# Clustered attention with two feed-forward blocks: tied clusters to the general path, four operand stacks, 15 fp32 probability steps, a new placement table

## The chip, the cores and the metric

The kernel runs on one core of one Trainium2 chip. The metric is device time in microseconds (us) of one execution, by the median of three runs.

## The reference

Sixteen heads (two batches of eight) of 768 tokens and 64 features go through attention in which a query sees only the keys of its own cluster. The result is the input of two feed-forward blocks.

```python
q_assign = np.argmax(einsum(q_n, c_n)); k_assign = np.argmax(einsum(k_n, c_n))   # 16 clusters
scores = np.where(q_assign == k_assign, (q @ k.T) / 8, -1e9)                     # 768 x 768 per head
attn = softmax(scores);  x = attn @ v                                            # (2, 768, 512)
u = x + real(fft2(x));  un = layernorm(u)
x = u + relu(un @ w_ch1) @ w_ch2                                                 # 512 -> 2048 -> 512
h = relu(x @ w_in);  out = (h * sigmoid(conv3(h))) @ w_out                       # 512 -> 1024 -> 512
```

`argmax` takes the first of several equal maxima.

## The kernel before, in words

The program holds the network twice. The fast path (`general=False`) runs first and computes a flag `fits` on the way (`heads_fit`, L692): the inputs' sizes lie in the ranges that its fp16 splits allow, and every query has a key in its cluster. If the flag is 0, the general path runs after it. All that follows is the fast path.

**Stages.** Attention with everything around it; the first feed-forward block for batch 0, then for batch 1; the second block. Values that need more than fp16 are split into a high and a low fp16 part, and a product is three matmuls (`pass3`).

**The attention loop** runs over 96 steps n, six per head: step n takes 128 keys of head n // 6 and all 768 queries. The query and key operands of a head, with 16 rows of cluster mask and a row for the maxima, lie in a pair of tiles X and Y, a *stack*. There are three stacks, used in turn (`Xs[h % 3]`). In program order a step does this:

- `score_max(n + LEAD)`, LEAD = 8: two matmuls make the scores of a step eight ahead (L1049, tile `s`), and VectorE takes the maximum of each row (L1056, `m6all`). When a head's six are there, `max_turn` (L1059) turns them round on TensorE, ScalarE scales them (L1064, `mr`), and a DMA puts them as one row into the head's stack (L1065, X<-mr). It is placed at step 6h - 2, two steps before the head h needs it.
- `score_exp(n)`: four matmuls make the transposed scores less the maxima (L1103 from X, L1105 from Y, tile `t`), ScalarE takes the exponential (L1112) into an fp32 tile `p`, of which there are three.
- `prob_hi(n - 1)` and `prob_lo(n - 1)`: the high part of p by a cast (ScalarE L1130, VectorE L1128 for steps in CAST_ON_DVE), the low part by a subtraction (GpSimd L1140, VectorE for steps in LO_ON_DVE).
- `attn_v(n - 4)`: 18 fp16 matmuls with the values (L1159). A *whole* step, by WHOLE = (2, 5) two steps of each head up to step 89, has no cast and no subtraction and takes six fp32 matmuls instead (L1152; the profile counts each twice). There are 29 of them; three more (IN_PLACE) leave p in PSUM.

The `s` and `t` tiles share three PSUM slots in turn (`slot`), so that TensorE can begin the next score only when VectorE's maximum or ScalarE's exponential has emptied an earlier one.

**Around the loop.** For each pair of heads m: loads (`load_raw`, `load_v`), the split of q and k (`prep_hi` L946, `prep_lo` L959, all on VectorE), similarity to the centroids (`prep_sims`), the maximum (L847) and a one-hot (L857) which holds several ones where clusters tie. For the first pair three VectorE operations pick the first of them (`prep_first` L861, `prep_pick` L865, `prep_mark` L871), for the other pairs two small matmuls with the matrix `sole` do (`equal_sole` L899, ScalarE L903, VectorE L906). The masks go to the stacks by way of DRAM (`equal_end`, `stack_mask`). From step 52 on the Fourier mixing of batch 0 (`mixing`, called stages `even0` to `ab2M`), its layer norm and the bits of four weight pieces (`ahead`) lie between the steps.

**What sets the order.** Every engine runs its instructions in the order in which the program issues them. The loop issues a step's parts in a fixed order, with lists between them (`pre`, `mid`, `mid2`, `late`, `aft`, `post`, `fill`); each small operation or load has a list and a step, and the table MOVED overrides these for 136 of them. All loads go out on SP's queue, those of the Fourier matrices (DFT_LOADS) on GpSimd's.

Of the kernel before, what the change touches and what calls it, by code (L numbers as in the profile page):

```python
# [23 lines left out]
DFT_LOADS = (9, 20, 21, 32, 33, 44)  # L24
# [154 lines left out]
    ('load_v', 1): ('late', 1),  # L179
    ('prep_lo', 1, 1): ('late', 1),  # L180
    ('stack_move', 2, 1, 2): ('aft', 2),
    ('v_step', 0, 4): ('aft', 2),
    ('v_step', 0, 6): ('pre', 3),
    ('prep_sims', 2): ('post', 5),
    ('prep_hi20', 2): ('fill', 6),
    ('equal_turn', 2): ('mid', 7),
    ('equal_sole', 2, 0): ('mid', 8),
    ('prep_hi21', 2): ('aft', 8),
    ('equal_sole', 2, 1): ('mid', 9),
    ('prep_lo', 2, 0): ('pre', 9),  # L190
    ('load_v', 2): ('fill', 10),
    ('attn_out', 0, 0): ('pre', 11),
    ('attn_out', 0, 1): ('pre', 11),
    ('prep_lo', 2, 1): ('late', 11),
    ('attn_out', 0, 2): ('fill', 12),
    ('load_raw', 3): ('aft', 12),
    ('v_step', 1, 6): ('pre', 12),
    ('v_step', 1, 4): ('late', 13),
    ('v_step', 1, 5): ('aft', 14),
    ('ahead_start', 0): ('aft', 15),  # L200
    ('ahead0_0',): ('aft', 16),
    ('ahead0_1',): ('fill', 16),
# [4 lines left out]
    ('v_step', 2, 6): ('late', 18),
    ('prep_hi31', 3): ('late', 20),
    ('v_step', 2, 5): ('late', 20),
    ('prep_hi30', 3): ('late', 21),  # L210
    ('attn_out', 2, 1): ('late', 22),
    ('prep_lo', 3, 1): ('pre', 22),
    ('prep_lo', 3, 0): ('late', 23),
    ('ahead0_3',): ('pre', 25),
    ('ahead_start', 1): ('aft', 25),
    ('ahead0_4',): ('fill', 26),
    ('attn_out', 2, 2): ('late', 26),
    ('ahead_split', 0, 0): ('fill', 27),
    ('ahead_store', 0): ('pre', 27),
    ('attn_out', 3, 0): ('aft', 27),  # L220
    ('ahead1_1',): ('fill', 29),
    ('attn_out', 3, 1): ('fill', 29),
    ('prep_sims', 4): ('post', 29),
    ('v_step', 3, 4): ('fill', 29),
    ('ahead1_2',): ('fill', 31),
    ('attn_out', 3, 2): ('fill', 31),
    ('v_step', 3, 5): ('pre', 31),
    ('prep_hi41', 4): ('fill', 32),
    ('prep_lo', 4, 0): ('late', 33),
    ('prep_lo', 4, 1): ('aft', 33),  # L230
    ('attn_out', 4, 1): ('aft', 34),
    ('ahead_start', 2): ('pre', 35),
    ('ahead1_3',): ('fill', 36),
    ('attn_out', 4, 2): ('aft', 36),
    ('ahead1_4',): ('pre', 37),
    ('ahead_split', 1, 0): ('pre', 39),
    ('attn_out', 5, 0): ('aft', 39),
    ('ahead2_0',): ('pre', 40),
    ('v_step', 4, 4): ('fill', 40),
    ('ahead2_1',): ('fill', 41),  # L240
    ('ahead_store', 1): ('fill', 41),
    ('attn_out', 5, 1): ('late', 41),
    ('prep_sims', 5): ('post', 41),
    ('v_step', 4, 6): ('pre', 42),
    ('v_step', 4, 5): ('fill', 43),
    ('prep_hi50', 5): ('pre', 44),
# [1550 lines left out]
```

## Time and profile before

| | us |
|---|---|
| runs of the kernel before | 668.8, 669.81, 675.71 |
| median | 669.81 |
| the profiled execution, its own time | 667.78 |
| its span, first to last instruction | 666.1 |
| around the span | 1.68 |
| TensorE busy in the span | 628.2 |
| VectorE, ScalarE, GpSimd busy | 482.0, 403.9, 121.4 |
| mean granted TensorE clock, of full speed | 0.983 |

In the rows below, PE is TensorE's matmuls, PEld its weight loads, DVE VectorE, ACT ScalarE, POOL GpSimd, SPq the queue of the loads. An arrow reads out<-in. A number in square brackets in a row of the timeline is the time for which the engine was idle before it and what ended that. A row of a stretch has the stretch's length, each engine's busy time in it with the number of instructions, then the granted clock (1.00 is 2.4 GHz, 0.50 is 1.2 GHz), the DMA engines' share and GB/s.

### The profile page before, as it was taken

The page shows a single profiled execution, that of the slowest core. Times are in us where ns is not written, and L with a number is a line of the kernel's source. Part 1 is how long each engine was busy: PE and PEld are TensorE (multiplying, and loading weights), DVE is VectorE, ACT ScalarE, POOL GpSimd, SP SyncE. Part 2 cuts the span into 40 slices and gives each one's busy share as a digit, 9 for nine tenths or more (in the row PEclk, how much of TensorE's full clock was granted, in tenths as well). Part 3 has the DMA queues.
Part 4 walks back from the last instruction along what each step waited for, and adds up shares of the span by engine and source line. Part 5 has one row for each costly group of instructions (what it writes and reads, how often), then busy time and mean ns, then how long its engine had stood idle before and what let it go on. Part 6 is the DMA issues. An engine that isn't in the chain of part 4 may idle for free.

```text
span 666.1 us, 11641 instructions
## 1 busy us (share of the span) xinstructions
PE 628.2 (94%) x4665; PEld 388.5 (58%) x4665; DVE 482.0 (72%) x814; ACT 403.9 (61%) x695; POOL 121.4 (18%) x108
## 2 busy tenths in 40 slices
PE   7799898898999999999999999999999999999995
PEld 3467676676877776565655555555555555555552
DVE  6988786979579998978789428777413489967663
ACT  6577586866477685787468514445413368886652
POOL 3252633644417631000020000000000000000000
PEclk9899798998999999999999999999999999999999
DMA  5445636554121610353034300333200002235202
GB/s 161 123 126 161 191 86 190 142 136 116 47 71 40 192 39 2 126 190 127 1 135 181 127 1 1 127 127 127 95 1 1 0 1 75 92 120 190 96 0 100
DMA packets 21943, 64.39 MB, mean 97 GB/s; under 512 B 7126, under 2 KB 8822, under 8 KB 19064
## 3 DMA queue, kind: packets, MB, share of 16 engines
q1 hardware_dynamic: 20872, 59.81, 28.3%
q0 software_dynamic: 1008, 3.75, 1.9%
q8 instruction: 38, 0.62, 0.4%
q14 instruction: 25, 0.20, 0.1%
HBM read 49.59 MB, written 4.89 MB: 82 GB/s over the span
## 4 chain that ended last, share of the span: by engine, by line
PE 61%; DVE 19%; ACT 12%; DMA 4%; issue 2%; ACTq 0%; DVEq 0%
PE acc L387 7%; PE acc L388 7%; PE acc L389 7%; DVE m6all L1056 5%; PE up L387 4%; PE up L389 4%; PE up L388 4%; PE av L1152 4%; PE t L1103 3%; DMA X<-mr 3%; PE t L1105 2%; PE av L1159 2%; PE s L1049 2%; PE u L387 2%; PE u L389 2%
## 5 line engine op out<-in xcount | busy, mean ns | idle before, releaser
L1112 ACT ACTIVATE p<-t,cbias 128x768 f32<-128x768 f32 x93 | 83.5, 899 | 44.7 <-PE t L1105 44.0
L1140 POOL TENSOR_TENSOR p<-p,p 128x768 f16<-128x768 f32 x47 | 84.9, 1812 | 126.0 <-DVE p L1128 69.7
L1056 DVE TENSOR_REDUCE m6all<-s 128x1 f32<-128x768 f32 x96 | 90.5, 948 | 23.4 <-PE s L1049 14.9
L387 PE MATMUL up<-un,wa 128*128 128x384 f16 x256 | 83.5, 326 | 1.9 <-DVE un L586 0.9
L389 PE MATMUL up<-un,wa 128*128 128x384 f16 x256 | 83.4, 326 | 0.0
L388 PE MATMUL up<-un,wa 128*128 128x384 f16 x256 | 83.4, 326 | 0.0
L1512 DVE SCALAR_TENSOR_TENSOR h<-up,h 128x384 f16<-128x384 f32 x62 | 33.6, 552 | 53.2 <-ACT h L1510 53.0
L387 PE MATMUL acc<-wa,h 128*128 128x512 f16 x186 | 70.6, 380 | 0.0
L388 PE MATMUL acc<-wa,h 128*128 128x512 f16 x186 | 70.5, 379 | 0.0
L389 PE MATMUL acc<-wa,h 128*128 128x512 f16 x186 | 70.5, 379 | 0.0
L1510 ACT ACTIVATE h<-up 128x384 f16<-128x384 f32 x62 | 29.9, 484 | 65.4 <-PE up L389 65.2
L1103 PE MATMUL t<-X 97*128 97x384 f16 x192 | 48.8, 336 | 14.4 <-DVE m6all L1056 8.1
L1159 PEld LDWEIGHTS <-p 128*128 128x128 f16 x1206 | 47.7, 100 | 9.6 <-issue 1.7
L1049 PE MATMUL s<-X 80*128 80x384 f16 x192 | 48.5, 336 | 4.9 <-DVE m6all L1056 4.0
L1159 PE MATMUL av<-V,p 128*128 128x65 f16 x1206 | 49.6, 197 | 0.0
L1105 PE MATMUL t<-Y 128*128 128x384 f16 x192 | 48.9, 337 | 0.0
L1152 PEld LDWEIGHTS av<-V,p 128*128 128x128 f32 x348 | 44.8, 200 | 2.0
L1152 PE MATMUL av<-V,p 128*128 128x65 f32 x348 | 44.2, 279 | 0.0
L387 PE MATMUL u<-x,wb 128*128 128x384 f16 x128 | 41.7, 326 | 0.2
L389 PE MATMUL u<-x,wb 128*128 128x384 f16 x128 | 41.7, 326 | 0.0
L388 PE MATMUL u<-x,wb 128*128 128x384 f16 x128 | 41.7, 326 | 0.0
L387 PE MATMUL acc<-wb,gH 128*128 128x512 f16 x96 | 36.4, 379 | 0.2 <-ACT gH L1548 0.2
(362 smaller groups left out, 1266.5 us busy)
## 6 DMA issues: line engine op xcount, KB each, us to landing
rawa<-w SPq DMA_DIRECT2D x14, 1024.0 KB, 5.4
rawb<-w SPq DMA_DIRECT2D x8, 1024.0 KB
heads<-qk SPq DMA_DIRECT2D x8, 768.0 KB, 5.2
raw<-qk SPq DMA_DIRECT2D x7, 768.0 KB, 6.7
Y<-G SPq DMA_DIRECT2D x27, 192.0 KB, 3.9
vraw<-v SPq DMA_DIRECT2D x8, 384.0 KB, 4.1
heads<-v SPq DMA_DIRECT2D x8, 384.0 KB, 4.2
out<-y SPq DMA_DIRECT2D x12, 256.0 KB, 4.4
```

Of the source, the lines that this page charges most:

```text
L387: T.matmul(o, sH, mH, start=start, stop=False)
L388: T.matmul(o, sH, mL, start=False, stop=False)
L389: T.matmul(o, sL, mH, start=False, stop=stop)
L1049: T.matmul(t[:, c, 0:384], X[0:80, 0, sl], X[0:80, 1, 384 * c:384 * c + 384], start=True, stop=True)
L1056: V.tensor_reduce(m6s[h][:, i:i + 1], t[:, :, 0:384], AX.XY, ALU.max, negate=True)
L1103: T.matmul(t[:, c, 0:384], X[0:rx, 1, sl], X[0:rx, 0, 384 * c:384 * c + 384], start=True, stop=False)
L1105: T.matmul(t[:, c, 0:384], Y[0:ry, k, sl], Y[0:ry, q, 384 * c:384 * c + 384], start=False, stop=True)
L1112: A.activation(p, t[:, :, 0:384], AF.Exp, bias=cbias[:, 0:1], scale=0.125 if general else 0.125 / QK_SCALE ** 2)
L1140: eng.tensor_sub(p16[:, 1], p, p16[:, 0])
L1152: T.matmul(avs[h][:, 65 * j:65 * j + 65], p[:, 128 * j:128 * j + 128], v32[:, WHOLE.index(i), h % 2], start=(i + j == 0), stop=(i == 5), s ...
L1159: T.matmul(o, p16[:, k, 128 * j:128 * j + 128], v16[:, i, h % 2, 65 * part:65 * part + 65], start=(i + j + k + part == 0), stop=(i == 5), ...
L1512: V.scalar_tensor_tensor(h[1][:, tk], o, 0.0, hh, ALU.max, ALU.subtract)
```

## The change

- **Ties.** The fast path no longer picks the first of tied clusters: `prep_first`, `prep_pick`, `prep_mark`, `equal_sole`, `desc` and `sole` go. The one-hot is turned and scaled straight to the mask by two ScalarE operations, the second of which sums its output (`ties`, by `accum_out`). `first_ties` does the sum for the first pair. `heads_fit` tests that the keys have exactly one cluster each, with one more matmul and four more VectorE operations of one column; otherwise `fits` is 0.
- **Four stacks** (`Xs[h % len(Xs)]`), and `prep_stack` may come earlier. `lead(n)` is 8, 9 from step 7 and 10 from step 19 (CATCH_UP), and `max_turn` moves with it, to the first n with n + lead(n) > 6h + 5.
- **WHOLE = (3,)**: 15 fp32 steps instead of 29; 14 more steps have a cast, a subtraction and 18 fp16 matmuls. The tile `pw` has 2 buffers instead of 4, `p16` 7 instead of 8, `raw` 2 instead of 1.
- **Engines.** Four of sixteen `prep_lo` go from VectorE to GpSimd (two operations each there), and the fp32 copy of v (`v_step` 6, now half as large) from ScalarE to GpSimd. Other steps stand in LO_ON_DVE and CAST_ON_DVE: 17 subtractions on VectorE as before, 61 on GpSimd for 47, 18 casts on VectorE for 22, 60 on ScalarE for 42.
- **Places.** MOVED is new, with 237 entries, and DFT_LOADS are at other steps.

```diff
-DFT_LOADS = (9, 20, 21, 32, 33, 44)
+DFT_LOADS = (2, 12, 25, 26, 29, 36)
...
-    ('prep_lo', 1, 1): ('late', 1),
+    ('prep_lo', 1, 1): ('aft', -7),
...
+LOW_ON_DVE = {0, 1, 4, 6, 7, 8, 9, 10, 11, 12, 13, 15}
+CATCH_UP = (7, 19)
...
-WHOLE = (2, 5)
+WHOLE = (3,)
...
+        T.matmul(o[:, 32:40], ones.to_broadcast([128, 128]), ties, start=True, stop=True)
...
-        V.scalar_tensor_tensor(r[:, 5:6].bitcast(I32), r[:, 2:3], most, r[:, 4:5], ALU.is_le, ALU.mult)
+        V.scalar_tensor_tensor(r[:, 6:7], r[:, 2:3], most, r[:, 4:5], ALU.is_le, ALU.mult)
+        V.tensor_scalar(r[:, 7:8], o[:, 32:33], 0.5 - 2 * S * (C - 1), None, ALU.is_le)
+        V.tensor_reduce(r[:, 0:1], o[:, 33:40], AX.X, ALU.max)
+        V.scalar_tensor_tensor(r[:, 7:8], r[:, 0:1], MASK_K * (0.5 - 2 * S * (C - 1)), r[:, 7:8], ALU.is_le, ALU.mult)
+        V.tensor_tensor(r[:, 5:6].bitcast(I32), r[:, 6:7], r[:, 7:8], ALU.mult)
...
+            if not general:
+                o = ohTs[m] = ep.tile([96, 2, 2, 128], F16, tag="ohT", bufs=1, name=f"ohT{m}")
+                o = o.rearrange("p a h n -> p a (h n)")
+                A.activation(o[:, 0], p[:, 0], AF.Copy, scale=MASK_Q)
+                A.activation(o[:, 1], p[:, 1], AF.Copy, bias=-MASK_K, scale=MASK_K, accum_out=ties[0:96, m:m + 1])
+                equal_end(m)
+                return
...
-                A.activation(V32s[m % 2][:, :, :, 0:64], src, AF.Copy, scale=V_SCALE)
+                G.tensor_scalar(V32s[m % 2][:, :, :, 0:64], src, V_SCALE, None, ALU.mult)
...
+        def first_ties():
+            e = eqs[0].rearrange("p (h a n) c -> p h a (n c)", h=2, a=2)[:, :, 1]
+            A.activation(e, e, AF.Copy, accum_out=ties[:, 0:1], bias=-1.0)
...
+        def lead(n):
+            return LEAD + (0 if general else sum(n >= c for c in CATCH_UP))
...
-                at(mid, 6 * h - 2, max_turn, h)
+                at(mid, next(n for n in range(100) if n + lead(n) > 6 * h + 5), max_turn, h)
...
+        if not general:
+            add_stack(G)
+            add_ones(G, 3)
...
-            tile_s = score_max(n + LEAD, mid.get(n, []))
+            for k in range(n + lead(n - 1), n + lead(n) + 1):
+                tile_s = score_max(k, mid.get(n, []) if k == n + lead(n) else [])
```

Three places show how the order moves. On ScalarE around the maxima of head 4 (`mr4`), whose first step is 24 (`p24`), the order was:

```order
L1112 ACTIVATE p20_954<-t20_949,cbias_72 128x768
L946 ACTIVATE G3_957<-raw3_700 128x768
L1112 ACTIVATE p21_995<-t21_990,cbias_72 128x768
L946 ACTIVATE G3_957<-raw3_700 128x768
L1064 ACTIVATE mr4_1012<-s30_1008 6x128
L1130 CAST p16_21_1016<-p21_995 128x768
L1112 ACTIVATE p22_1023<-t22_1018,cbias_72 128x768
L1130 CAST p16_22_1050<-p22_1023 128x768
L1112 ACTIVATE p23_1057<-t23_1052,cbias_72 128x768
L1112 ACTIVATE p24_1094<-t24_1089,cbias_72 128x768
```

On the same engine it now is:

```order
L1178 ACTIVATE mr4_963<-s30_959 6x128
L1248 CAST p16_19_967<-p19_947 128x768
L1230 ACTIVATE p20_974<-t20_969,cbias_72 128x768
L1248 CAST p16_20_999<-p20_974 128x768
L1230 ACTIVATE p21_1006<-t21_1001,cbias_72 128x768
L1230 ACTIVATE p22_1041<-t22_1036,cbias_72 128x768
L1248 CAST p16_22_1068<-p22_1041 128x768
L1230 ACTIVATE p23_1075<-t23_1070,cbias_72 128x768
L1139 ACTIVATE V16_0_139<-vraw2_904 128x12x64
L712 ACTIVATE ahead_668,cbias_72<-ahead_668 128x512
L1230 ACTIVATE p24_1115<-t24_1110,cbias_72 128x768
```

Two exponentials (p22, p23) stood between `mr4` and `p24`; now four do (p20 to p23).

On GpSimd in the middle of the loop (`p16_36` is the low part of step 36, DC and OD the Fourier matrices) the order was:

```order
L1140 TENSOR_TENSOR p16_36_1512<-p36_1497,p16_36_1512 128x768
L1140 TENSOR_TENSOR p16_37_1544<-p37_1519,p16_37_1544 128x768
L1140 TENSOR_TENSOR p16_39_1601<-p39_1582,p16_39_1601 128x768
L1140 TENSOR_TENSOR p16_40_1637<-p40_1608,p16_40_1637 128x768
L1140 TENSOR_TENSOR p16_42_1715<-p42_1696,p16_42_1715 128x768
L1140 TENSOR_TENSOR p16_43_1754<-p43_1722,p16_43_1754 128x768
L1448 DMA DC_80<-dft 128x1032
L1450 DMA OD_81<-odd 128x644
```

There it now is:

```order
L1258 TENSOR_TENSOR p16_37_1594<-p37_1571,p16_37_1594 128x768
L1258 TENSOR_TENSOR p16_38_1634<-p38_1601,p16_38_1634 128x768
L1258 TENSOR_TENSOR p16_40_1710<-p40_1684,p16_40_1710 128x768
L1258 TENSOR_TENSOR p16_41_1742<-p41_1717,p16_41_1742 128x768
L1258 TENSOR_TENSOR p16_42_1786<-p42_1749,p16_42_1786 128x768
L1258 TENSOR_TENSOR p16_43_1812<-p43_1793,p16_43_1812 128x768
L1258 TENSOR_TENSOR p16_44_1849<-p44_1819,p16_44_1849 128x768
L1129 TENSOR_SCALAR V32_0_145<-vraw4_1294 128x2x64
L1258 TENSOR_TENSOR p16_46_1916<-p46_1889,p16_46_1916 128x768
```

Four of six steps had a subtraction on GpSimd; here five of six do, and the copy of v (V32) stands between them.

On VectorE before the first maxima (`m6all` of `s0`; the first pair's one-hot is `eq0`) the order was:

```order
L857 TENSOR_TENSOR eq0_197<-cols0_172,mx0_195 128x384
L861 TENSOR_TENSOR eq0_197<-eq0_197,desc_109 128x384
L865 TENSOR_REDUCE m20_223<-eq0_197 128x24
L871 TENSOR_TENSOR oh0_225<-desc_109,m20_223 128x384
L847 TENSOR_REDUCE mx1_228<-sim1_217 128x24
L926 TENSOR_SCALAR X0_138<-fm01_231 16x384 x2
L857 TENSOR_TENSOR early_99<-sim1_217,mx1_228 128x384
L959 SCALAR_TENSOR_TENSOR G0_169<-raw0_102,G0_169 128x768 x2
L1056 TENSOR_REDUCE m6all_166<-s0_271 128x1
```

There it now is:

```order
L968 TENSOR_TENSOR eq0_179<-cols0_155,mx0_177 128x384
L958 TENSOR_REDUCE mx1_205<-sim1_199 128x24
L1040 TENSOR_SCALAR X0_121<-fm01_208 16x384 x2
L968 TENSOR_TENSOR early_100<-sim1_199,mx1_205 128x384
L1073 SCALAR_TENSOR_TENSOR G0_152<-raw0_103,G0_152 128x768 x2
L1170 TENSOR_REDUCE m6all_149<-s0_248 128x1
```

Three operations between the one-hot and what follows are gone.

## Rows read from the trace of the kernel before

**Rows 1.** The stretches: before the first exponential, the loop, its tail, the first block.
```profile
0.00:21.55 21.55, 16.27 (x106) 7.65 (x107) 16.24 (x51) 12.10 (x21) 6.56 (x24) 1.00 0.46 144
21.55:243.68 222.13, 202.04 (x2168) 153.09 (x2168) 181.51 (x269) 153.77 (x229) 103.46 (x74) 0.95 0.43 123
243.68:258.10 14.42, 14.01 (x220) 10.60 (x220) 10.80 (x19) 8.85 (x13) 4.94 (x3) 1.00 0.01 3
258.10:365.00 106.90, 103.53 (x579) 61.21 (x577) 90.35 (x135) 75.67 (x141) 5.70 (x6) 1.00 0.33 117
```
**Rows 2.** The page's chain that ended last, share of the span by engine.
```profile
PE 61%; DVE 19%; ACT 12%; DMA 4%; issue 2%; ACTq 0%; DVEq 0%
```
**Rows 3.** The waits of TensorE: us in total, times, longest us.
```profile
PE t L1103 <- DVE m6all L1056: 8.1, 14, 1.9
PE t L1103 <- DMA X<-mr: 5.1, 4, 2.0
```
**Rows 4.** The timeline: the maxima's DMA, and matmuls that waited longest.
```profile
70.32 0.77 SPq L1065 DMA_DIRECT2D X<-mr  x1
...
75.38 0.50 PE L1103 MATMUL t<-X 97*128 97x384 f16 x2 [1.97 <-DMA X<-mr]
...
105.39 0.50 PE L1103 MATMUL t<-X 97*128 97x384 f16 x2 [1.56 <-DMA X<-mr]
...
161.32 0.48 PE L1103 MATMUL t<-X 97*128 97x384 f16 x2 [1.94 <-DVE m6all L1056]
```
**Rows 5.** Four stretches at the lower clock, in the columns of rows 1.
```profile
28.60:32.10 3.50, 3.40 (x27) 2.17 (x28) 2.43 (x5) 1.89 (x3) 0.67 (x1) 0.51 0.07 15
76.40:83.50 7.10, 7.10 (x53) 5.05 (x53) 2.85 (x4) 2.82 (x4) 2.89 (x2) 0.52 0.63 213
107.10:110.60 3.50, 3.50 (x29) 2.41 (x29) 1.42 (x2) 1.63 (x4) 0.72 (x1) 0.51 1.07 238
161.80:169.00 7.20, 7.20 (x45) 6.11 (x43) 3.37 (x5) 2.63 (x3) 4.71 (x6) 0.53 0.81 272
```
**Rows 6.** The timeline of TensorE over two steps, an fp16 and an fp32 one.
```profile
51.75 0.49 PE L1049 MATMUL s<-X 80*128 80x384 f16 x2
...
53.28 0.49 PE L1049 MATMUL s<-X 80*128 80x384 f16 x2
...
54.27 1.45 PE L1152 MATMUL av<-V,p 128*128 128x65 f32 x12
55.55 0.33 PE L1049 MATMUL s<-X 80*128 80x384 f16 x1
```
**Rows 7.** The timeline elsewhere: tie matmuls, and VectorE behind the test of sizes.
```profile
152.38 0.28 PE L899 MATMUL s<-eT,sole 96*96 96x128 f16 x2
...
655.81 0.75 DVE L1571 TENSOR_SCALAR y<-acc,ysc 128x512 f32<-128x512 f32 x1 [1.31 <-PE acc L389]
```
**Rows 8.** Single lines: count, shortest, median, longest ns; first and last start.
```profile
L1140 POOL TENSOR_TENSOR p<-p,p x47: 1633/1647/2362, 24.7 to 251.5; 128x768 f16<-128x768 f32 x47
...
L1128 DVE CAST p<-p x22: 546/550/1357, 24.0 to 250.4; 128x768 f16<-128x768 f32 x22
...
L959 DVE SCALAR_TENSOR_TENSOR G<-raw,G x14: 942/958/1940, 12.3 to 197.5; 128x768 f16<-128x768 f32 x14
```
**Rows 9.** Groups of instructions: busy us, mean ns of one; idle us before them.
```profile
L1130 ACT CAST p<-p 128x768 f16<-128x768 f32 x42 | 34.5, 822 | 0.4
...
L906 DVE TENSOR_SCALAR ohT<-s 96x256 f16<-96x256 f32 x6 | 2.5, 413 | 0.0
...
L1015 ACT ACTIVATE V<-vraw 128x256 f32<-128x256 f32 x8 | 3.3, 406 | 0.0
```
**Rows 10.** The timeline of VectorE and ScalarE before the first exponential.
```profile
9.08 0.36 DVE L861 TENSOR_TENSOR eq<-eq,desc 128x384 f16<-128x384 f16 x1
9.47 0.55 DVE L865 TENSOR_REDUCE m<-eq 128x24 f16<-128x384 f16 x1
10.06 0.56 DVE L871 TENSOR_TENSOR oh<-desc,m 128x384 f16<-128x384 f16 x1
10.55 0.56 DVE L847 TENSOR_REDUCE mx<-sim 128x24 f32<-128x384 f32 x1
```
**Rows 11.** The stretch of the Fourier matmuls, in the columns of rows 1.
```profile
162.40:204.30 41.90, 40.39 (x369) 32.60 (x368) 29.52 (x46) 25.45 (x42) 16.57 (x12) 0.93 0.30 88
```

More of the change, by code (lines that the diff above doesn't have):

```diff
@@ L207 @@
[L207 to L234, printed above, removed]
@@ new lines @@
+    ('stat', 1): ('post', 75),
+    ('attn_out', 11, 0): ('pre', 76),
+    ('low', 0): ('late', 76),
+    ('swap', 0): ('late', 76),
+    ('ab2M',): ('late', 77),
+    ('attn_out', 11, 1): ('pre', 77),
+    ('prep_stack', 15): ('post', 77),
+    ('scale', 3): ('pre', 78),
+    ('stat', 4): ('post', 78),
+    ('low', 3): ('aft', 79),
+    ('root', 1): ('fill', 79),
+    ('stat', 2): ('late', 79),
+    ('swap', 3): ('late', 79),
+    ('v_step', 7, 4): ('fill', 79),
+    ('attn_out', 11, 2): ('post', 81),
@@ L768, in tile_net @@
         V.memset(W, 0.0)
-        desc = ep.tile([128, C], F16, name="desc")
-        for c in range(C):
-            V.memset(desc[:, c:c + 1], float(C - c))
-        sole = ep.tile([96, NT, C], F16, name="sole")
-        G.memset(sole, -1.0)
+        if general:
+            desc = ep.tile([128, C], F16, name="desc")
+            for c in range(C):
+                V.memset(desc[:, c:c + 1], float(C - c))
+            sole = ep.tile([96, NT, C], F16, name="sole")
+            G.memset(sole, -1.0)
+        else:
+            G.memset(ties, 0.0)
         t = slot("warm_up")
@@ L1205, in tile_net @@
             at(fill, load, load_v, m)
-            if general:
-                at(aft, top, v_max, m)
-                at(mid, turn_v, v_turn, m)
-            for i in range(4 if general else 0):
+            at(aft, top, v_max, m)
+            at(mid, turn_v, v_turn, m)
+            for i in range(4):
                 if i:
@@ L1245, in tile_net @@
         for h in range(NH):
-            if h > 2:
-                pre.setdefault(6 * (h - 2), []).insert(0, (prep_stack, h))
             if h:
-                at(mid, 6 * h - 2, max_turn, h)
+                at(mid, next(n for n in range(100) if n + lead(n) > 6 * h + 5), max_turn, h)
             for i in range(3):
                 at(fill, 6 * h + 5 + LAG + (h > NH - 3) + i, attn_out, h, i)
+        for h in range(NH - 1, 2, -1):
+            place = "pre", 6 * (h - 2) if general else 4 if h == 3 else 6 * h - 15 - 3 * (h % 2)
+            where, n = (MOVED_GENERAL if general else MOVED).get(("prep_stack", h), place)
+            hooks[where].setdefault(n, []).insert(0, (prep_stack, h))
         def two(name):
```

418 lines of the change are left out of this document (274 added, 144 removed).

## The prediction

> **What bounds the kernel now.** I read the busy time by stretches first. Up to the first exponential at 21.55 us VectorE is the busiest engine beside TensorE. In the loop, to 243.68 us, TensorE is busy 202.0 of 222.1 us, VectorE 181.5, ScalarE 153.8, GpSimd 103.5, and the mean clock is 0.95 of 2.4 GHz. Behind the loop TensorE is busy all but 3.4 of the 106.9 us up to 365 [rows 1]. The diff touches nothing that runs after 258 us but the test of the flag, so I take the later stages to keep their length and move earlier by what the attention gains. Next I read the chain that ended last: 61% of the span is on TensorE, 19% on VectorE, 4% on DMA [rows 2]. Third, TensorE's own waits: it stood 8.1 us for VectorE's maxima and 5.1 us, four times, for the DMA of the maxima, X<-mr [rows 3]. One such DMA is issued at 70.32 and the matmul that needs it starts at 75.38, after 1.97 us of idleness [rows 4]. So a DMA of 5 us faces two steps of some 2 us.
>
> Last, the clock. It stood at 1.2 GHz in four stretches, of 3.5, 7.1, 3.5 and 7.2 us, with means of 0.51 to 0.53 [rows 5]. At half speed a stretch loses half its length to TensorE, and (1 - clock) x length gives 1.7, 3.4, 1.7 and 3.4, together 10.2 us. What came before: the second and third follow waits of 1.97 and 1.56 us for X<-mr, the fourth a wait of 1.94 us for VectorE's maximum [rows 4, 5]. So a wait for X<-mr can cost its idle time and then again as much or twice as much.
>
> **Term 1, the beginning: -1.9 us.** The three operations that pick the first of tied clusters run from 9.08 to 10.55 on VectorE, and the next maximum stands right behind them [rows 10]: 1.5 us. The mask operation of the next pair, 0.41 by the like row [rows 9], also stands between the maxima for which the first exponential waits. VectorE has no gap in these rows, so I take all of it, 1.9, and 0 as the other bound, should ScalarE's copies or the loads end later than VectorE does now.
>
> **Term 2, work taken from TensorE and VectorE in the loop: -10 us.** An fp16 step takes TensorE from 51.75 to 53.28, 1.53 us, an fp32 step from 53.28 to 55.55, 2.27 us [rows 6]. The difference is 0.74, and 14 steps change: 10.4 us. The 28 tie matmuls go: a pair spans 0.28 us [rows 7], so they cost 14 x 0.28 = 3.9 us at most and, as matmuls overlap, rather less: I take 1.6. TensorE has 12 us less to do. VectorE loses four splits of 0.96, four casts of 0.55 [rows 8] and six mask operations of 0.41 [rows 9]: 3.8 + 2.2 + 2.5 = 8.5 us. As scores and maxima share three PSUM slots, the loop follows whichever of the two is behind. Both fall, one by 12 and the other by 8.5. I take 10, and keep 8.5 and 12 as its ends.
>
> **Term 3, the maxima's DMA: -6 us.** `max_turn` of heads 4 to 15 moves from two steps before its use to four, of heads 2 and 3 to three; head 1's stays. Two more steps are at least 2 x 1.53 = 3.1 us, and the longest of the four waits was 2.0 [rows 3, 6]. Against it: its queue is ordered, and whole loads of q and k are now issued right ahead of it at heads 1 and 4. The four waits are 5.1 us, and two of them led to low-clock stretches worth 3.4 + 1.7 = 5.1 us more. The bounds are 0 (another wait takes their place) and -10.2 (all of it). I take the idle time and a fifth of the clock, 5.1 + 1 = 6, since other gaps can lower the clock as well.
>
> **Term 4, what is added: +2 us.** Fourteen casts and four that leave VectorE come to ScalarE, 18 x 0.82 = 14.8 us, less eight copies of 0.41 = 3.3 [rows 9]. That is 11.5 on an engine with 153.8 of 222.1 us busy [rows 1], and it then stands at some 165 of 206: covered, though an exponential can be late by one cast. The two ScalarE operations in place of a copy and a Relu per pair I set at nothing. GpSimd gets 14 subtractions of 1.65 us (23 us), four splits of two operations (at most 8 x 1.65 = 13 us) and eight copies, a sixth of such a tile each (0.3 us, an estimate from 128 of 768 columns): about 38 us, so 142 of some 206. What is queued behind a late subtraction is the next one; `attn_v` waits for the low part and the exponential three steps on for the buffer of p. With 5 x 1.65 = 8.3 us a head beside 5 x 1.53 + 2.27 = 9.9 us on TensorE that is covered, and at the longest subtraction seen, 5 x 2.36 = 11.8, it is not [rows 8].
>
> That longest subtraction points to a cost that no count of instructions holds. The rows spread: subtractions on GpSimd take 1.65 in the median and 2.36 at most, casts on VectorE 0.55 and 1.36, splits there 0.96 and 1.94 [rows 8]. The medians lie at the minima, so most operations meet nothing. If each of the 22 added GpSimd operations lengthened one VectorE operation by 0.8 (1.36 less 0.55), that were 17.6 us. I take half of it, 8, as the upper bound for the loop, 0 as the lower, and 2 as the value, nearer to the median rows. [...]
>
> **At no cost:** five more small operations in the test of the flag, some 0.7 us. VectorE waits 1.31 us for TensorE right behind the old ones [rows 7], which hides them; uncovered they would cost that 0.7. The fourth stack's clearing is on GpSimd before the loop. The first weight loads are now issued behind the last maxima; the tail of the loop, 14.4 us in which the DMA engines have a share of 0.01 [rows 1], covers them, and what came later than that would be late by as much.
>
> **Sum.** -1.9 - 10 - 6 + 2 = -15.9. The profiled execution took 667.78 (666.1 of span and 1.68 around it), 2.0 below the median of 669.81. From the median the forecast is 653.9, so 654 us.
>
> **Rivals.**
> First, everything comes off: -1.9 - 12 - 10.2 + 0 = -24.1, so 646 us. For it speaks that the waits for X<-mr are short beside the time that the move gives; against it that VectorE, with 8.1 us of waits on it, gets less relief than TensorE.
> Second, GpSimd and VectorE get in each other's way, and the waits stay in another form: -1.9 - 8.5 - 0 + 6 = -4.4, so 665 us. For it: five subtractions a head where four stood, and the spread of rows 8. Against it: GpSimd would still be idle a third of the loop.
> Third, slower: the clock stays low in the stretch of the Fourier matmuls, 162.4 to 204.3 us. TensorE is busy 40.4 of 41.9 us there at a clock of 0.93, so its work at full clock is about 37.5 us [rows 11]; the table moves more of VectorE's steps of the mixing and of the weight bits into these steps. Should waits like the one of 1.94 us recur so that the clock stays at half through it, the stretch takes 75 us, 33 more; with the gains before it, -15.9 + 33 = +17, 687 us. It decides from the point where the clock is low for 38 us in all, 16 more lost than now. Against it: it was low for 7.2 us of this stretch.
> Fourth, the change does not do what it says: the sums count a tie in these data, the flag is 0 and the general path runs after the fast one. A second network at no less than the first's 653 gives 1,300 us or more. Equal fp32 maxima in random data speak against it.
>
> **How the numbers follow.** Forecast 0.56, first rival 0.18, second 0.18, third 0.06, fourth 0.02. A measurement here can tell 1% from no change, that is, 663 to 676.5. The forecast and the first rival lie below, and a little of the second, 0.05: faster 0.79. The rest of the second is 0.13 within. Slower is 0.08. Best ends of all terms give 646, and 642 if the other two low-clock stretches go in part; the worst ends (-8.5 + 8, nothing else) give about 669. The range is 642 to 668.
>
> **What would show it.** Right: the first exponential at about 19.6 us; no wait of TensorE for X<-mr from head 4 on; at most two low-clock stretches in the loop; the loop some 206 us long and the later stages as long as now. Wrong: TensorE waiting for the exponential or for the low part; the median of GpSimd's subtractions well above 1.65; the clock at half between 150 and 200 us for more than 10 us; instructions of the general path in the trace.

## The result, and the profile after

The changed kernel takes 637.29 us in the median of four runs (637.15 to 637.56), the kernel before 671.99 beside it (668.8 to 675.71). The ratio is 0.948, with a 95% interval of 0.942 to 0.954. The forecast was 654 with a range of 642 to 668: the direction was right, the gain was 34.7 us where 15.9 had been worked out, and the time lies below the range. Of the 34.7 us, 2.2 are the kernel before, which measured 671.99 here and 669.81 where the forecast was counted from.

The profiled execution took 637.15 us, 30.6 less than that of before, and its span is 635.4. The stretches of the changed kernel are first the four of [rows 1] with its own ends (the beginning, the loop, its tail, the first block), then its two stretches at the lower clock, which answer to [rows 5].

```profile
0.00:24.24 24.24, 20.05 (x103) 8.39 (x104) 15.18 (x30) 12.95 (x25) 14.22 (x27) 0.84 0.56 174
24.24:213.22 188.98, 180.18 (x2236) 133.79 (x2235) 172.17 (x252) 162.25 (x244) 144.28 (x101) 0.98 0.47 129
213.22:228.10 14.88, 14.88 (x217) 11.46 (x214) 11.39 (x23) 8.83 (x13) 4.77 (x3) 1.00 0.30 122
228.10:335.00 106.90, 103.77 (x580) 61.25 (x579) 90.95 (x136) 76.42 (x143) 5.70 (x6) 1.00 0.33 118
16.30:26.50 10.20, 10.00 (x34) 3.91 (x33) 7.66 (x9) 3.89 (x10) 6.44 (x5) 0.50 0.73 210
81.10:84.50 3.40, 3.40 (x27) 2.09 (x26) 2.23 (x4) 2.69 (x6) 0.99 (x1) 0.50 0.64 163
```

The beginning got 2.7 us longer, the loop 33.1 shorter (222.1 to 189.0), the tail 0.5 longer, and what follows the attention took 407.9 us before and 407.3 after. So the loop holds the whole effect. GpSimd's share in it rose from 103 of 222 to 144 of 189 us, and TensorE now stands idle for 8.8 us of it instead of 20.1. The chain that ended last, by engine, against [rows 2]:

```profile
PE 69%; DVE 17%; ACT 10%; issue 2%; DMA 1%; DVEq 0%; ACTq 0%
```

TensorE's waits inside the loop, in the columns of [rows 3]: the wait for X<-mr is gone, the one of `t` for VectorE's maxima fell from 8.1 to 1.7, and a new one stands first, for the one-hot of a new pair (`eq`).

```profile
PE s L1163 <- DVE eq L968: 3.9, 3, 2.3
PE t L1221 <- DVE m6all L1170: 1.7, 5, 0.6
PE t L1221 <- DVE YcL L569: 1.1, 1, 1.1
PE s L1175 <- DVE m6all L1170: 0.7, 2, 0.4
```

Single lines of the changed kernel, against [rows 8]: count, shortest, median and longest ns of GpSimd's subtractions, of V's low split on VectorE, and of VectorE's maxima.

```profile
L1258 POOL TENSOR_TENSOR p<-p,p x61: 1639/1651/2360, 26.1 to 218.8; 128x768 f16<-128x768 f32 x61
...
L1141 DVE SCALAR_TENSOR_TENSOR V<-vraw,V x8: 950/1179/2596, 25.8 to 206.3; 128x768 f16<-128x768 f32 x8
...
L1170 DVE TENSOR_REDUCE m6all<-s x96: 887/949/958, 14.3 to 204.1; 128x1 f32<-128x768 f32 x96
```

The split takes up to 2.7 times its shortest time; the maximum, which reads PSUM, takes 0.89 to 0.96 us throughout. To compare kernels I call *excess* what VectorE's instructions in the loop take above the shortest one of the same line and shape in any of the traces, summed up: 20.3 us before and 20.9 after, of 195.1 and 186.3 us of instructions. (The expectations below have figures up to 0.6 lower, from fewer traces.) The shortest times alone add up to 174.8 before and 165.4 after. Not all of the excess is collision: in each kernel 5.1 to 5.6 us of it are the 87 maxima in the loop, which take 0.95 us where the shortest of all took 0.89. So differences of the excess count, and not its level.

The table has the loop of each kernel told of here, in us. Work is TensorE's busy time less what the clock cost; clock is half the length of the stretches at a granted clock of 0.50; idle is the length less the busy time. The three add up to the loop. Half, because in the kernel before two score matmuls of 384 columns each take 0.33 us from start to start of the next two at a granted clock of 1.00 (45.02 to 46.00 us) and 0.64 at 0.50 (78.14 to 80.06). These paces, 2.4 and 1.2 columns a ns, are what the traces show of the GHz that stand beside the clock above. The kernels stood beside the kernel before on several chips, where its medians were 667.72 to 671.99 us, so a difference between medians taken on different chips is good to some 4 us. One execution of before_halfpool (669.39) was in the slow state, and without it that kernel's median is 659.73.

| kernel | median | loop | work | clock | idle | excess on VectorE |
|---|---|---|---|---|---|---|
| before | 671.99 | 222.1 | 191.8 | 10.2 | 20.1 | 20.3 |
| after | 637.29 | 189.0 | 177.4 | 2.8 | 8.8 | 20.9 |
| b_whole1 | 671.71 | 225.5 | 185.4 | 5.1 | 35.1 | 30.9 |
| whole2 | 650.98 | 202.0 | 188.5 | 0 | 13.5 | 27.0 |
| oldtable | 677.70 | 230.9 | 180.0 | 15.4 | 35.5 | 38.4 |
| oldrest | 675.49 | 226.9 | 180.0 | 13.7 | 33.2 | 35.0 |
| oldprep | 672.29 | 223.6 | 180.0 | 8.5 | 35.1 | 31.2 |
| lead8 | 652.18 | 206.3 | 176.4 | 9.7 | 20.2 | 25.7 |
| before_halfpool | 661.26 | 216.5 | 191.2 | 8.3 | 17.0 | 12.3 |
| b_whole1_halfpool | 660.67 | 211.4 | 184.8 | 1.7 | 24.9 | 15.9 |
| old_halfpool | 654.94 | 208.8 | 182.2 | 1.7 | 24.9 | 14.9 |
| lead8_halfpool | 645.44 | 200.7 | 176.3 | 6.8 | 17.6 | 15.1 |
| after_halfpool | 636.06 | 188.4 | 177.3 | 1.7 | 9.4 | 14.8 |
| warm2 | 633.88 | 187.7 | 178.0 | 0 | 9.7 | 22.0 |

From before to after the loop's 33.1 us are 14.4 of work, 7.4 of clock and 11.3 of idle time. Work is not exact: for the same matmuls as in the changed kernel it reads from 176.3 (lead8_halfpool) to 182.2 (old_halfpool), so its differences are good to some 3 us. The experiments ask where the clock and the idle time come from.

### The profile page after: what moved, and what is told of

It is laid out like the page before. It is cut to its first block, busy times and chain, and to the rows that moved or that the text cites. A ratio compares the mean times of both kernels' runs of the same rounds, so it can differ in the third digit from the quotient of the medians.

```text
span 635.4 us, 11809 instructions
## 1 busy us (share of the span) xinstructions
PE 610.6 (96%) x4723; PEld 370.6 (58%) x4723; DVE 472.5 (74%) x784; ACT 413.3 (65%) x714; POOL 169.7 (27%) x137
## 4 chain that ended last, share of the span: by engine, by line
PE 69%; DVE 17%; ACT 10%; issue 2%; DMA 1%; DVEq 0%; ACTq 0%
PE acc L490 7%; PE acc L492 7%; PE acc L491 7%; PE av L1277 5%; PE up L490 5%; PE up L492 5%; PE up L491 5%; PE t L1221 4%; DVE m6all L1170 4%; PE t L1223 4%; PE s L1163 4%; PE av L1270 2%; PE u L490 2%; PE u L492 2%; PE u L491 2%
## 5 line engine op out<-in xcount | busy, mean ns | idle before, releaser
L1258 POOL TENSOR_TENSOR p<-p,p 128x768 f16<-128x768 f32 x61 | 108.3, 1785 | 41.7 <-DVE p L1246 15.0
L1170 DVE TENSOR_REDUCE m6all<-s 128x1 f32<-128x768 f32 x96 | 90.2, 949 | 12.3 <-PE s L1163 10.1
L1230 ACT ACTIVATE p<-t,cbias 128x768 f32<-128x768 f32 x93 | 83.2, 897 | 15.1 <-PE t L1223 14.4
L1277 PEld LDWEIGHTS <-p 128*128 128x128 f16 x1458 | 55.0, 98 | 12.0 <-issue 3.3
L1277 PE MATMUL av<-V,p 128*128 128x65 f16 x1458 | 58.2, 194 | 0.0
L1248 ACT CAST p<-p 128x768 f16<-128x768 f32 x60 | 49.5, 825 | 0.9
L670 POOL TENSOR_TENSOR rs<-rs,half 128x1 f32<-128x1 f32 x12 | 10.0, 833 | 100.0 <-DVE rs L665 82.7
```

The lines of the kernel that those rows point to most:

```text
L1170: V.tensor_reduce(m6s[h][:, i:i + 1], t[:, :, 0:384], AX.XY, ALU.max, negate=True)
L1230: A.activation(p, t[:, :, 0:384], AF.Exp, bias=cbias[:, 0:1], scale=0.125 if general else 0.125 / QK_SCALE ** 2)
L1248: A.copy(p16[:, 0], p32s[n])
L1258: eng.tensor_sub(p16[:, 1], p, p16[:, 0])
L1277: T.matmul(o, p16[:, k, 128 * j:128 * j + 128], v16[:, i, h % 2, 65 * part:65 * part + 65], start=(i + j + k + part == 0), stop=(i == 5), ...
```

## The experiments

Three theories stood at the start: A, the longer lead of scores and maxima; B, the new places of the small operations; C, the smaller work itself. Each kernel was timed beside the kernel before on the same chip, and ratios are to that one.

**The lead alone taken back: lead8.**

```diff
-CATCH_UP = (7, 19)
+CATCH_UP = ()
```

> The changed kernel with the lead of scores and maxima kept at 8 steps throughout (CATCH_UP empty); four stacks and the new table stay. Theory A (the vanished waits come from the lead: with 10 steps the maxima are there long before their use): the waits for X<-mr and for m6all come back in part, 8 to 15 us, and with them one or two stretches of low clock; 648 to 655 us. Theory B (they come from where the small operations are placed): 638 to 642 us, hardly any wait for X<-mr. Theory C (they come from the smaller work of TensorE and VectorE): as B.

Measured: 652.18 us (646.67 to 654.78), ratio 0.971 (0.964 to 0.978). The lead is worth 15 us, and a good part of that comes by way of the clock: the executions of lead8 took 646.67 us at a mean clock of 0.989 and 654.28 at 0.975. The loop, and three of TensorE's waits in it:

```profile
24.25:230.57 206.32, 186.12 (x2236) 137.07 (x2235) 177.35 (x252) 163.94 (x243) 141.64 (x101) 0.95 0.46 126
...
PE t L1221 <- DVE m6all L1170: 9.2, 12, 3.3
PE s L1163 <- DVE eq L968: 3.0, 4, 1.8
...
PE t L1221 <- DMA X<-mr: 0.4, 1, 0.4
```

Theory A's time came true, its wait for X<-mr did not: that took 0.4 us, once. The lead removes waits for the maxima themselves.

**The places taken back: oldtable, oldrest, oldprep.** All three are the changed kernel with entries of MOVED (and defaults) replaced by the places of the kernel before: all of them (oldtable, lead 8), those of V's split, outputs, weight bits, mixing and norm (oldrest, lead as changed), and those of what prepares the scores (oldprep, lead 8). The instructions and their engines are those of the changed kernel, and so are LO_ON_DVE, CAST_ON_DVE, LOW_ON_DVE and DFT_LOADS. So the old places meet sets and loads that were not chosen for them; no run tells how much of the loss is this mismatch. The lead and three entries of oldtable, whose stacks are also loaded where they were (step 6(h - 2)):

```diff
-CATCH_UP = (7, 19)
+CATCH_UP = ()
...
-    ('v_step', 2, 5): ('pre', 27),
+    ('v_step', 2, 5): ('late', 20),
...
-    ('attn_out', 2, 2): ('post', 23),
+    ('attn_out', 2, 2): ('late', 26),
...
-    ('prep_lo', 2, 0): ('pre', 5),
+    ('prep_lo', 2, 0): ('pre', 9),
```

> The changed kernel (ties, stacks, one fp32 step a head, the same choice of engines) with every operation and load that both tables place at the place of the kernel before, and a lead of 8. Theory A: as lead8, 648 to 655 us. Theory B: the waits for the maxima of the kernel before come back, some 10 us with 5 to 8 us of clock on top of the lead: 655 to 662 us. Theory C: 645 to 650 us, the loop above that of the changed kernel by the X<-mr waits alone.

Measured: 677.70 us (675.44 to 680.57), ratio 1.011 (1.005 to 1.017). The other edits, without the new places and the longer lead, make the kernel no faster, rather 1% slower, which is above what any of the theories said. TensorE's work did fall, by 11.8 us, but its idle time rose to 35.5 and the excess on VectorE to 38.4. One place in the timeline of oldtable shows how:

```profile
58.50 1.55 DVE L1255 CAST p<-p 128x768 f16<-128x768 f32 x1 [0.74 <-ACT p L1239]
...
59.98 4.30 DVE L1150 SCALAR_TENSOR_TENSOR V<-vraw,V 128x768 f16<-128x768 f32 x1
...
60.21 3.24 POOL L1267 TENSOR_TENSOR p<-p,p 128x768 f16<-128x768 f32 x2
...
64.20 0.94 DVE L1179 TENSOR_REDUCE m6all<-s 128x1 f32<-128x768 f32 x1
...
65.20 0.37 PE L1184 MATMUL s<-ident,m6all 128*6 128x128 f32 x1 [4.09 <-DVE m6all L1179]
```

A split of 0.95 us takes 4.30, that is 3.35 more, beside two subtractions of GpSimd that take 3.24 together. A maximum is queued behind it, TensorE stands 4.09 us, and the granted clock is 0.50 from 62.3 to 69.1, by the row of this stretch in the columns of [rows 1]:

```profile
62.30:69.10 6.80, 3.90 (x28) 2.45 (x29) 6.42 (x9) 2.00 (x3) 3.09 (x3) 0.50 0.44 139
```

The longest cast of oldtable takes 2.16 us where the shortest takes 0.54, which is 1.62 more, about one subtraction of 1.65. So by their sizes the lost times are about one and two subtractions of GpSimd. What makes the VectorE instruction wait, and which of the two starts first, the trace does not show: the split is recorded at 59.98, ahead of the subtractions, which start at 60.21.

> The changed kernel with its lead and its places for what prepares the scores (loads of q and k, high and low parts, ties, stacks), but with the places of the kernel before for the rest (V's split, outputs of attention, weight bits, mixing, norm). If the excess on VectorE comes from this rest: 655 to 670 us, with an excess of 30 us or more. If it is the places of the preparation and the lead that count: 638 to 648 us.

Measured: 675.49 us (674.91 to 676.08), ratio 1.011, excess 35.0, above the 655 to 670 that was expected if this rest carries the excess. New places for the preparation, with the lead, give nothing alone.

> The fourth corner beside oldtable, oldrest and the changed kernel: the places of the kernel before, and its lead of 8, for what prepares the scores, the new places for the rest. If the rest alone carries the effect (by keeping VectorE's instructions out of GpSimd's way): 645 to 656 us, near lead8, with an excess on VectorE of 20 to 27 us. If the two halves of the table only work together: 665 to 678 us, with an excess of 30 us or more.

Measured: 672.29 us (669.52 to 678.03), ratio 1.007, excess 31.2. New places for the rest give nothing alone either. With both halves at lead 8 (lead8) it is 652. So the two halves of the table work together only. The excess of both fits that what is left in an old place meets GpSimd's work again; these two runs do not show it by themselves.

The loops of the two, oldrest and then oldprep:

```profile
23.02:249.94 226.92, 193.69 (x2236) 139.66 (x2235) 186.66 (x256) 164.10 (x244) 140.32 (x101) 0.94 0.42 116
```

```profile
24.92:248.55 223.63, 188.50 (x2236) 136.53 (x2235) 182.73 (x252) 162.77 (x243) 141.67 (x101) 0.96 0.42 117
```

**GpSimd's instructions halved: old_halfpool, after_halfpool, lead8_halfpool.** This tests the collision itself. Only the first half of the low part of p is computed on GpSimd, and TensorE uses it twice, so its work stays and the result leaves out half of GpSimd's low parts.

```diff
-                eng.tensor_sub(p16[:, 1], p, p16[:, 0])
+                e = S if eng is V or general else S // 2
+                eng.tensor_sub(p16[:, 1, 0:e], p[:, 0:e], p16[:, 0, 0:e])
...
-                    T.matmul(o, p16[:, k, 128 * j:128 * j + 128], ...
+                    jj = j % 3 if k and not general else j
+                    T.matmul(o, p16[:, k, 128 * jj:128 * jj + 128], ...
```

> The kernel of oldtable, but GpSimd's subtractions of the low part of p work on 384 of 768 columns, and TensorE reads the first half of the low part twice; VectorE's own subtractions are whole. TensorE, ScalarE and VectorE have the same instructions. Theory P (with the old places VectorE loses its time beside GpSimd: in oldtable its instructions in the loop take 205.1 us where the shortest of each kind add up to 167.1): the excess of 38 us falls to 20 or less, the loop gets 10 to 18 us shorter, 660 to 668 us. Rival Q (the old places are bad because instructions stand in the wrong order and wait for one another): the time stays at 674 to 680 us.

Measured: 654.94 us (652.44 to 656.34), ratio 0.978, 22.8 below oldtable, with an excess of 14.9. This is more than theory P said, and rival Q falls. The loop is 22.1 us shorter: 13.7 of the clock and 10.6 of idle time, against 2.2 more of work. Another reading, that the low parts simply come sooner, has little room: in oldtable's loop ScalarE waited 3.3 us for GpSimd's subtractions and TensorE 0.2 us, in a weight load. Its loop, the split and the maxima:

```profile
23.78:232.56 208.78, 183.86 (x2236) 133.78 (x2236) 168.06 (x256) 163.95 (x245) 97.11 (x101) 0.99 0.46 130
...
L1150 DVE SCALAR_TENSOR_TENSOR V<-vraw,V x8: 947/957/1673, 28.2 to 201.8; 128x768 f16<-128x768 f32 x8
...
L1179 DVE TENSOR_REDUCE m6all<-s x96: 895/950/959, 15.5 to 227.2; 128x1 f32<-128x768 f32 x96
```

and the split and the maxima of oldtable:

```profile
L1150 DVE SCALAR_TENSOR_TENSOR V<-vraw,V x8: 950/1540/4300, 29.2 to 223.7; 128x768 f16<-128x768 f32 x8
...
L1179 DVE TENSOR_REDUCE m6all<-s x96: 895/949/960, 15.4 to 250.5; 128x1 f32<-128x768 f32 x96
```

The split is the same instruction in both; only GpSimd's neighbours got shorter. In oldtable's loop six of the eight splits overlap an instruction of GpSimd, and the other two take 0.95 us.

> The changed kernel with the same halved subtractions on GpSimd. Theory P: its excess on VectorE is 20.5 us of 186.3, but TensorE waits for VectorE only 7.7 us in its loop, so the gain is small beside that of old_halfpool: 0 to 6 us, 631 to 637 us. Rival Q: 635 to 638 us.

Measured: 636.06 us (635.52 to 637.85), ratio 0.952, the same as the changed kernel within the noise (637.29, and 636.25 in after2 below). With the new places and the long lead the same collisions cost next to nothing, though 20.9 us of excess are there.

> The kernel of lead8 (new places, lead of 8) with GpSimd's subtractions halved as in old_halfpool. If the longer lead is worth its 15 us only because VectorE is late now and then beside GpSimd: 636 to 642 us, near after_halfpool. If the lead is worth as much without that: 647 to 652 us.

Measured: 645.44 us (643.05 to 647.51), between the two. The lead is worth 652.18 - 637.29 = 14.9 us with the collisions and 645.44 - 636.06 = 9.4 with the short subtractions. By these sums about a third of its gain is cover for a VectorE made late by collisions, and the rest it has without them. The same sum for the places, at a lead of 8: 677.70 - 652.18 = 25.5 with the collisions, 654.94 - 645.44 = 9.5 with short ones and an equal excess (14.9 and 15.1). By these sums some 16 us of the places' gain are collisions; the rest I put down to where the instructions stand in VectorE's queue, which no run tests by itself. Much of the 16 comes by way of the clock: with its cost taken off the loops of the table, the places are worth 18.9 us with the collisions and 13.2 without. These sums add single kernels from several chips, so each is good to a few us. Nor do the parts add up: lead, places and fp32 steps, each taken back, cost 14.9, 25.5 and 13.7 us (whole2, below), together more than the whole gain.

**One fp32 step a head: whole2, b_whole1 and the halved pair.** whole2 is the changed kernel with two fp32 steps a head again, b_whole1 the kernel before with one.

```diff
-WHOLE = (3,)
+WHOLE = (2, 5)
...
-                src = vraws[m][:, WHOLE[0]:WHOLE[0] + 1]
+                src = vraws[m][:, WHOLE[0]::WHOLE[1] - WHOLE[0]]
...
-            p16 = probs[n] = ap.tile([128, 2, S], F16, tag="p16", bufs=5 if general else 7, name=f"p16_{n}")
+            p16 = probs[n] = ap.tile([128, 2, S], F16, tag="p16", bufs=5 if general else 6, name=f"p16_{n}")
```

> The changed kernel with two fp32 steps a head again (WHOLE = (2, 5), and 6 instead of 7 buffers of p16 for space). TensorE gets 14 times 0.74 = 10.4 us more, VectorE and GpSimd less. Theory C (the work counts in full and with it waits): 649 to 656 us. If the work of TensorE alone counts: 646 to 649 us. If TensorE's time were hidden: 637 to 641 us.

Measured: 650.98 us (649.84 to 653.23), 13.7 above the changed kernel. TensorE's work rises by 11.1 us (10.4 expected) and its idle time by 4.7, and the clock's cost falls by 2.8: the work counts in full, as theory C said.

> The kernel before with one fp32 step a head (WHOLE = (3,)) and nothing else of the change. Theory C: TensorE saves 10.4 us and the time falls by 8 to 14 us, to 657 to 663. Theories A and B: the steps get faster but the waits for maxima and for X<-mr grow, since VectorE and GpSimd have more to do at the old places: 664 to 672 us.

Measured: 671.71 us (670.21 to 675.64), ratio 1.002 (0.996 to 1.008). In the kernel before the same edit gains nothing. Its loop, and its casts and low parts on VectorE (22 and 17 in the kernel before):

```profile
23.33:248.85 225.52, 190.47 (x2263) 137.98 (x2263) 199.98 (x283) 158.81 (x236) 117.26 (x81) 0.98 0.44 121
...
L1128 DVE CAST p<-p x29: 539/551/1889, 25.7 to 255.5; 128x768 f16<-128x768 f32 x29
...
L1140 DVE TENSOR_TENSOR p<-p,p x24: 941/954/1539, 30.3 to 251.5; 128x768 f16<-128x768 f32 x24
```

The old sets of engines give VectorE seven casts and seven subtractions of the freed steps, 7 x 0.55 + 7 x 0.95 = 10.5 us, and the excess rises by 10.6. VectorE is busy 200 of 225.5 us there, and TensorE's saving turns into waits: by the table work falls by 6.4 and the clock's cost by 5.1, and the idle time rises by 15.0.

> The kernel before with GpSimd's subtractions halved. Its excess on VectorE is 19.8 us and TensorE waits 13 us for maxima. If the excess was a cost before the change already: 652 to 661 us. If TensorE bounds it as its profile says: 664 to 670 us.

> The kernel before with one fp32 step a head (as b_whole1, which did not get faster) and GpSimd's subtractions halved. If TensorE's 10.4 us were lost there to VectorE's excess (30.5 us, 10.7 above that of the kernel before): 6 to 11 us below before_halfpool. If they are lost to something else, such as VectorE's seven added casts and subtractions: within 4 us of before_halfpool.

Measured: 661.26 us (657.57 to 669.39, ratio 0.983, 0.978 to 0.988) and 660.67 (657.57 to 666.29, ratio 0.988, 0.981 to 0.995). The kernel before already paid some 8 to 12 us for the collisions. With them shortened, one fp32 step still gains nothing, though the two differ in excess by 3.6 us only: the added excess is not what takes TensorE's saving. By elimination it is the 10.5 us of added instructions on VectorE; no run takes these away alone. The changed kernel's sets put no more of them on VectorE than before, which may be a part of why the edit pays there.

**The low clock at the beginning: warmvs, warm2, warm2vs, after2.** Idle fp16 matmuls of 128 columns are put behind the first score tiles, and V's split of pair 2 (2.60 us at 76.32 in the changed kernel, ahead of the wait of 2.29) is moved.

```diff
-    ('v_step', 2, 5): ('pre', 27),
+    ('v_step', 2, 5): ('post', 24),
...
+                    T.matmul(tile_s[:, 1, 384:512], zero[:, 0:128], zero[:, 0:128], start=True, stop=True)
```

> The changed kernel with two additions against its two stretches of low clock: four idle fp16 matmuls of 128 columns behind each of the first six score tiles (into columns of the tile that nobody reads), so that TensorE has no gaps between 12 and 17 us, and V's low split of pair 2 moved from step 27 to step 24, away from the maxima of a new pair, where TensorE waited 2.29 us. If the gaps bring the low clock on: the stretches at 16.3 and 81.1 us go, the wait of 2.29 us goes, 637.3 - 5.1 - 1.7 - 2 = 628 to 633 us. If the low clock comes anyway, or elsewhere: 635 to 641 us.

Measured: 646.67 us (645.96 to 650.17), 9 us slower than the changed kernel. The idle matmuls wrote into spare columns of the score tile, and each group of four waited for that tile's maximum, the first 2.27 us and the other five 1.05 each. The first in the timeline:

```profile
14.92 0.58 PE L1579 MATMUL s<-early 128*128 128x128 f16 x4 [2.27 <-DVE m6all L1170]
```

The first exponential came at 32.6 us, and the granted clock was 0.50 from 14.5 to 31.5. As TensorE's gaps were still there, this run does not test whether they bring on the low clock. The moved split brought no gain in the loop (190.0 us).

> The changed kernel with four idle fp16 matmuls of 128 columns behind each of the first six score tiles, this time into a PSUM tile that nothing else uses, so that they wait for nothing (in warmvs they waited for the maximum of the tile they wrote into). If TensorE's gaps between 12 and 17 us bring on the low clock of 16.3 to 26.5 us: first exponential at 19 to 20.5 us, 632 to 634 us. If it comes anyway: 637 to 640 us.

```diff
+        idle = None if general else ps.tile([128, 512], F32, tag="av", bufs=2, name="idle")
         for n in range(-LEAD, 6 * NH + 11):
...
+            if not general and n in range(-8, -2):
+                for _ in range(4):
+                    T.matmul(idle[:, 0:128], zero[:, 0:128], zero[:, 0:128], start=True, stop=True)
```

```diff
-    ('v_step', 2, 5): ('pre', 27),
+    ('v_step', 2, 5): ('late', 27),
```

> As warm2, and V's low split of pair 2 behind the maxima of the new pair in step 27 (it stood ahead of them, and TensorE waited 2.29 us for them). If the wait and the low clock at 81 us go with it: 2 to 4 us below warm2. If the wait only moves: the same as warm2.

> The changed kernel once more, on the chip of warm2 and warm2vs, for comparison: 636 to 639 us.

Measured on one chip: after2 636.25 us (635.73 to 637.2; ratio 0.952, 0.945 to 0.959), warm2 633.88 (632.39 to 635.67; 0.949, 0.941 to 0.956), warm2vs 634.64 (633.52 to 635.74). The granted clock of the beginning stays at 1.00 in warm2 and in warm2vs, while the first exponential of warm2, at 21.15, is later than the 19 to 20.5 expected. In warm2 no stretch of the attention falls to the lower clock (1.00 in both rows below), that of the changed kernel at 81.1 included, although the wait of 2.3 us for `eq` is still there. Its beginning and loop:

```profile
0.00:21.15 21.15, 17.42 (x127) 8.91 (x128) 14.24 (x30) 12.94 (x24) 13.16 (x27) 1.00 0.58 179
21.15:208.80 187.65, 177.99 (x2236) 132.58 (x2236) 173.84 (x253) 162.02 (x244) 144.83 (x102) 1.00 0.48 134
```

So 24 matmuls that compute nothing make the fastest kernel here, by 2.4 us. The four runs of each do not overlap, but only just (635.67 and 635.73), and the intervals of the ratios do. Two runs of warm2 took 632.4 us at mean clocks of 0.996 and 0.998, the other two 635.3 and 635.7 at 0.993; only one of the first two was profiled. Moving the split as well moves the wait: TensorE then waits 1.6 us for V itself, and the granted clock falls at 78.9 (its mean over the loop is 0.99).

## Why the prediction was wrong

In the profiled executions the span fell by 30.6 us where 15.9 had been worked out. Terms 1 and 2 miss by 4.6 and 4.4 us in opposite directions, and that they cancel is luck. The 14.7 us that are missing stand in terms 3 and 4, which gave -4 together where the loop's idle time and clock gave -18.7.

- **Term 1, the beginning (-1.9): wrong in sign, +2.7.** The time that the removed operations left on VectorE became a wait there. The next maximum (`mx`) needs `sim` from TensorE, which waits for ScalarE's copy `st` (done at 10.05), stands behind seven matmuls that compute nothing (`warm`), and comes at 10.32; `mx` waits 1.50 us for it and starts at 10.85, where it started at 10.55 before [rows 10]. TensorE's transposes for the mask (`fm`) stand behind `sim` as well. They started at 10.67 before, after 0.16 us of waiting for `oh`, and start at 10.74 now. So TensorE's first score tile, which waits for ScalarE's copy of the mask, starts at 12.53 for 12.46. That VectorE had no gap in the rows of before did not make it the engine that the others waited for. The text kept a bound of 0, for ScalarE's copies or the loads; it was ScalarE's copy and TensorE's queue. The rows of the changed kernel:

```profile
8.80 1.68 PE L891 MATMUL warm<-early 128*128 128x512 f16 x7
10.32 0.49 PE L949 MATMUL sim<-ident,st 128*128 128x128 f32 x3
10.74 1.51 PE L1034 MATMUL fm<-ident,eq 128*16 128x128 f16 x24
...
10.85 0.56 DVE L958 TENSOR_REDUCE mx<-sim 128x24 f32<-128x384 f32 x1 [1.50 <-PE sim L949]
...
11.68 0.80 ACT L1045 ACTIVATE X<-fm 16x768 f16<-16x768 f16 x1 [0.88 <-PE fm L1034]
12.53 0.82 PE L1163 MATMUL s<-X 80*128 80x384 f16 x4 [0.28 <-ACT X L1045]
```

  On top came the clock, granted at 0.50 from 16.3 to 26.5 us, which at half speed costs TensorE 4 us before the first exponential. In warm2, without it and with the idle matmuls, the first exponential is at 21.15, 0.4 us before that of the kernel before. No row of before could show this stretch, since its clock was full (1.00) up to 28.6 us in that execution; in b_whole1, which begins with the instructions of the kernel before, it was low from 15.4 to 22.3 (mean 0.85 up to the first exponential at 23.33).
- **Term 2, work (-10): the mechanism held, the size was 2 to 4 us short.** TensorE's work fell by 14.4 us from before to the changed kernel, and by 11.8 in oldtable with the same matmuls. The text had 10.4 for the steps and up to 3.9 for the tie matmuls, 14.3, then took 1.6 of the 3.9 and cut the sum to 10 because VectorE gains less. VectorE's shortest times fell by 9.4, against the 8.5 worked out, and yet TensorE's saving counted in full. I put that down to the lead of 10 steps, with which VectorE may be late now and then without TensorE noticing; no run takes the lead and the fp32 steps back together. b_whole1 shows the limit that I had in mind, in the kernel before.
- **Term 3, "the maxima's DMA: -6 us": this is the step that failed.** It priced the lead and the early `max_turn` by the waits for X<-mr alone, and counted a fifth of the clock. TensorE waited 13.0 us in the loop for VectorE's maxima (8.1 in [rows 3], and 3.3 and 1.6 for the matmuls of `s` and of the turn). They stood in the trace and got no term. The two lines of the kernel before that [rows 3] leaves out:

```profile
PE s L1049 <- DVE m6all L1056: 3.3, 6, 1.2
PE s L1061 <- DVE m6all L1056: 1.6, 3, 1.2
```

  After the change 2.4 are left; the X<-mr waits are gone, other waits of some 4 us are new, and the clock gives back 7.4 us where 1 was taken. lead8 shows that the lead is worth 15 us at the new places: in its loop the wait of `t` for the maxima is 7.5 us longer than in the changed kernel and the clock costs 6.9 more, while its X<-mr wait is 0.4.
- **Term 4, added load (+2): about right by its size, and still misjudged.** The excess rose by 0.6 us, and ScalarE and GpSimd made nobody wait for long. But the upper bound of 8 was for these instructions in any place, and in the old places they raise the excess by 18.1 (oldtable). I priced GpSimd's instructions by their number; what decides is which instruction of VectorE stands beside them and what is queued behind it. MOVED, the largest part of the change, had no term, and without it and the lead there is no gain at all.
- **The rivals.** The first, "everything comes off" (646), was nearest, and its -24.1 is still 10 short since it has no term for the maxima either. The second, collisions between GpSimd and VectorE (665), names the mechanism that oldtable shows, at 677.70; in the changed kernel the new places and the lead make it nearly free. The granted clock stayed at 1.00 from 84.5 us to the end of the loop at 213.2, and so in the Fourier stretch, and no general path ran.
- **What was to show it.** Right: no wait for X<-mr, at most two low stretches in the loop, later stages as long as before. Wrong: the first exponential (24.24, not 19.6) and the loop (189, not 206). None of the signs listed for a wrong prediction appeared; all of them watched for a slower kernel.

Open is how the collisions, the place in the queue and the clock share the gain of the new table beyond the sums above, and how much of the loss in old places comes from sets and loads that were chosen for the new ones.

## What to carry to other kernels

When two engines collide, a table of places is a change of its own: price it by the long instances of a line (longest beside shortest) and by what is queued behind each, and not by added instructions. Give every wait of the bounding engine a term, that for the maxima too, since here the longer lead took most of them off together (the wait of `t` is 9.2 us in lead8 and 1.7 with it). Before moving work from the bounding engine, see that it does not come to the one that is next (b_whole1). An engine without gaps is not yet the one that holds up the others: ask what its next instruction waits for once the one before it is gone (term 1).

## What the runs showed of the hardware

- In oldtable VectorE's casts took 0.54 to 2.16 us and V's two-input splits 0.95 to 4.30, up to 1.62 and 3.35 more than the shortest, where one subtraction of GpSimd takes 1.65 and two 3.24. The 96 maxima, which read PSUM, stay between 0.89 and 0.96 us in all three traces shown, although 63 of the 87 in oldtable's loop overlap an instruction of GpSimd. The norm's statistics, which read SBUF, do not stretch either: 0.65 to 0.70 us in oldtable (L670, 12 times), and 0.68 to 0.70 in the changed kernel (L661), where seven of the 12 overlap an instruction of GpSimd. What spares these two kinds no run here separates. Halving GpSimd's subtractions lowered the excess from 38.4 to 14.9 us.
- The clock of the beginning is not the same in every execution of a kernel: the changed kernel had 10.2 us at a granted clock of 0.50 in one profiled execution and 3.4 (17.8 to 21.2) in the other. With 24 idle matmuls that wait for nothing it stayed at 1.00 in the traces of both (warm2, warm2vs); of the kernels without them only the kernel before showed that in its trace.
